# A linear-attention state gram by single heads on four column quarters of the TensorE array, with the projections around it on quarters too

## The chip, the cores and the metric

The kernel runs on one core of a Trainium2 chip. The metric is the device time of one execution in microseconds (us). A core has engines that run side by side and meet at semaphores: TensorE (PE, matmuls; PEld, its weight loads), VectorE (DVE), ScalarE (ACT), GpSimd (POOL) and SyncE (SP), which here issues most transfers. Sixteen DMA engines move the data.

## The reference, cut to what matters

Sequence 2048, width 640, 32 heads of 20. The output is a gated mix of a linear attention with a learned feature map and a GEGLU feed-forward.

```python
q, k, v = (x @ wqkv) split into 32 heads of 20
pk = k @ w_phi                                   # per head, 20 x 20; the same for q
phi_k = concat(softmax(pk), softmax(-pk))        # 40 features
kv = einsum("bhsf,bhsd->bhfd", phi_k, v)         # the state: per head 40 x 20, summed over 2048 tokens
z  = sum over tokens of phi_k
o  = (phi_q @ kv) / (phi_q @ z + 1e-6)
a  = o @ wo
b  = (gelu(x @ w_gate) * (x @ w_up)) @ w_down
out = g * a + (1 - g) * b                        # g = sigmoid(sum(x * gate_w))
```

The state gram is what changes: `kv` and `z` together, for each tile of 128 tokens the product of 21 columns (20 of v, one of ones) by 40 features per head, accumulated over 16 tiles.

## The kernel before: the parts that matter

In the "column stage", from the first gram to the last, every matmul with 128 output rows is issued as two of 64 rows, on the two column halves of the array. The halves stream at the same time (in the trace each starts a matmul of N=512 every 215.5 ns). The gram is on halves too, three heads in one matmul (so most of its output is other heads' cross terms, never used):

```python
def mm(self, bank, c0, n, lhs, rhs, first, fin, reads):      # all projections and gate/up products
    for a, z in ((0, 64), (64, P)) if self.columns else ((0, P),):
        ... e.matmul(self.ps[a:z, bank*512+c0 : ...+n], lhs[:, a:z], rhs, ...)

def gram_groups(self):                                       # 11 groups of 3 heads (the last of 2)
    fe = 3 * self.DH
    for g in range(11):
        u = g // 2
        yield (g, 64 * (g % 2), 3 + u // 4, 2 * fe * (u % 4), ..., fe * g, min(fe, self.D - fe * g))

def gram(self, t):
    ...
    for g, a, b, c, lo, f0, nf in self.gram_groups():
        ... e.matmul(self.ps[a:a+64, b*512+c : ...+2*nf], va[:, lo:lo+64], self.Ek[:, se, :, f0:f0+nf], ...)
```

One step of the stage projects a tile of 128 tokens (v, k and a gate column), makes one 512-wide product for q, and takes the gram of the tile three steps back. VectorE normalises the softmax of k (`k_norm`) meanwhile.

The softmax here doesn't subtract the row's maximum and nothing guards it: scores larger than these inputs give would overflow.

## Time and profile before

| | before |
|---|---|
| time, median of 4 runs | 286.5 us (286.4 to 287.05) |
| span of the profiled run | 285.0 us |
| PE busy | 281.1 us, 99% |
| first gram to the first recorded full-width matmul after the last gram | 28.44 to 84.44, 56.00 us |
| a steady step (one token tile, one gram) | 4.09 us |
| DMA engines | full until about 45 us (feed-forward weights from 23 us on), then nearly idle |

PE is the bottleneck from end to end, so time taken from it anywhere should come off the total. The next fence is the chain of waits of the kernel before in order of time, in a steady step (start, us, what). L361 is `mm`, L468 the gram.

```profile
52.04 0.27 PE ps L468 x8
52.30 0.05 PE ps L361
52.35 0.04 PE ps L468
52.39 3.73 PE ps L361 x37
56.12 0.27 PE ps L468 x8
```

The chain goes from matmul to matmul with nothing between, 4.08 us from gram to gram, of which the gram has about 0.3. A single matmul of the gram lasts 215 ns in the groups by shape, but matmuls are pipelined, and it is the distance of starts that tells its cost: 52.5 ns on one half for N=120, 35 ns for N=80.

Last, what follows the stage: in the timeline, the state's copies out of PSUM on VectorE (L482) and ScalarE (L484), and the next two gelus (L653):

```profile
85.64 1.34 DVE L482 CAST Ek<-ps 64x480 bf16<-64x480 f32 x2
87.08 0.82 ACT L484 ACTIVATE Ek<-ps 64x120 bf16<-64x120 f32 x3 [2.46 <-DVE Ek L482]
87.80 1.06 ACT L653 ACTIVATE gl<-ps 128x512 bf16<-128x512 f32 x2
```

### The profile page before, as it was taken

The page shows a single profiled execution, that of the slowest core. Times are in us where ns is not written, and L with a number is a line of the kernel's source. Part 1 is how long each engine was busy: PE and PEld are TensorE (multiplying, and loading weights), DVE is VectorE, ACT ScalarE, POOL GpSimd, SP SyncE. Part 2 cuts the span into 40 slices and gives each one's busy share as a digit, 9 for nine tenths or more (in the row PEclk, how much of TensorE's full clock was granted, in tenths as well). Part 3 has the DMA queues.
Part 4 walks back from the last instruction along what each step waited for, and adds up shares of the span by engine and source line. Part 5 has one row for each costly group of instructions (what it writes and reads, how often), then busy time and mean ns, then how long its engine had stood idle before and what let it go on. Part 6 is the DMA issues. An engine that isn't in the chain of part 4 may idle for free.

```text
span 285.0 us, 7066 instructions
## 1 busy us (share of the span) xinstructions
PE 281.1 (99%) x3045; PEld 186.1 (65%) x3060; DVE 174.4 (61%) x352; ACT 105.2 (37%) x200; POOL 5.3 (2%) x36
## 2 busy tenths in 40 slices
PE   8999999999999999999999999999999999999996
PEld 4665799999984444444444444445777777777786
DVE  1459999999976652667242334225883883883801
ACT  4367898667754223222322223221112112112021
POOL 7000000000000000000000000000000000000000
DMA  8999993000002000011000000000233223322421
GB/s 228 225 199 313 361 349 111 2 0 2 2 0 48 0 0 2 2 23 25 0 0 0 2 0 0 0 2 0 26 82 58 50 62 59 70 52 68 71 72 48
DMA packets 36937, 18.67 MB, mean 66 GB/s; under 512 B 28970, under 2 KB 36394, under 8 KB 36906
## 3 DMA queue, kind: packets, MB, share of 16 engines
q1 hardware_dynamic: 36240, 18.19, 26.3%
q8 instruction: 24, 0.39, 0.6%
q10 hardware_dynamic: 666, 0.03, 0.2%
q14 instruction: 7, 0.06, 0.1%
HBM read 9.04 MB, written 2.62 MB: 41 GB/s over the span
## 4 chain that ended last, share of the span: by engine, by line
PE 99%; issue 0%; ACT 0%
PE ps L361 62%; PE ps L737 28%; PE ps L681 2%; PE ps L373 2%; PE ps L468 2%; PE ps L341 1%; PE ps L557 1%; PE ps L298 0%; ACT outsb L750 0%; PE ps L564 0%; PE ps L323 0%
## 5 line engine op out<-in xcount | busy, mean ns | idle before, releaser
L361 PE MATMUL ps<-xT,wg_sb 128*128 128x512 bf16 (+1 forms) x265 | 63.8, 379 | 0.4 <-issue 0.2
L361 PE MATMUL ps<-xT,wu_sb 128*128 128x512 bf16 (+1 forms) x263 | 63.3, 379 | 0.4
L653 ACT ACTIVATE gl<-ps 128x512 bf16<-128x512 f32 x52 | 30.9, 596 | 72.9 <-PE ps L361 70.7
L655 DVE TENSOR_TENSOR hT<-ps,gl 128x512 bf16<-128x512 f32 x39 | 26.6, 689 | 38.8 <-PE ps L361 38.7
L737 PE MATMUL ps<-wd_sb,hT 64*128 64x320 bf16 x648 | 48.5, 296 | 0.0
L361 PEld LDWEIGHTS ps<-xT,wu_sb 128*128 128x128 bf16 (+1 forms) x270 | 26.6, 99 | 29.5
L361 PEld LDWEIGHTS ps<-xT,wg_sb 128*128 128x128 bf16 (+1 forms) x270 | 26.2, 99 | 29.0 <-ACT gl L653 0.2
L361 PE MATMUL ps<-w,xT 128*64 128x512 bf16 (+6 forms) x398 | 41.5, 325 | 0.1
L750 ACT ACTIVATE outsb<-ps,Gm 128x320 bf16<-128x320 f32 (+2 forms) x31 | 14.5, 515 | 72.4 <-PE ps L737 72.4
L737 PEld LDWEIGHTS ps<-wd_sb,hT 64*128 64x128 bf16 x648 | 31.1, 94 | 12.2 <-issue 0.4
L361 PEld LDWEIGHTS ps<-w,xT 128*64 128x64 bf16 (+1 forms) x400 | 35.9, 107 | 4.5
L737 PE MATMUL ps<-wo_sb,goT 64*128 64x320 bf16 (+2 forms) x340 | 26.5, 288 | 0.0
L361 PE MATMUL ps<-xT,wq 128*64 128x512 bf16 (+1 forms) x184 | 26.0, 380 | 0.1
L438 DVE TENSOR_REDUCE Dk<-Ek 128x64 f32<-128x1280 bf16 x16 | 23.7, 1478 | 3.7 <-ACT gcol L426 3.7
L452 DVE TENSOR_TENSOR Ek<-Ek,Dk 128x640 bf16<-128x640 bf16 x32 | 25.0, 821 | 0.6
L708 DVE TENSOR_TENSOR O<-ps,RH 128x640 bf16<-128x640 f32 x32 | 24.7, 815 | 0.0
L423 ACT ACTIVATE Ek<-ps 128x640 bf16<-128x640 f32 x32 | 20.7, 703 | 4.2 <-PE ps L361 4.2
L537 ACT ACTIVATE Eq<-ps 128x512 bf16<-128x512 f32 x40 | 21.6, 607 | 0.6 <-PE ps L361 0.4
L655 DVE TENSOR_TENSOR xT<-ps,gl 128x512 bf16<-128x512 f32 x13 | 9.0, 690 | 18.2 <-PE ps L361 18.2
L737 PEld LDWEIGHTS ps<-wo_sb,goT 64*128 64x128 bf16 x340 | 16.0, 94 | 5.3
L361 PEld LDWEIGHTS ps<-xT,wq 128*64 128x64 bf16 (+1 forms) x185 | 15.4, 108 | 2.9
L737 PE MATMUL ps<-wd_sb,xT 64*128 64x320 bf16 (+2 forms) x270 | 16.0, 269 | 0.0
(71 smaller groups left out, 173.8 us busy)
## 6 DMA issues: line engine op xcount, KB each, us to landing
out_dram<-outsb SPq DMA_DIRECT2D x7, 320.0 KB, 2.3
wd_sb<-in_B_w_down_dram SPq DMA_DIRECT2D x1, 2080.0 KB, 12.9
wg_sb<-in_B_w_gate_dram SPq DMA_DIRECT2D x1, 1120.0 KB, 7.4
wu_sb<-in_B_w_up_dram SPq DMA_DIRECT2D x1, 1120.0 KB, 9.8
wg_sb<-in_B_w_gate_dram SPq DMA_DIRECT2D x1, 960.0 KB, 9.1
wu_sb<-in_B_w_up_dram SPq DMA_DIRECT2D x1, 960.0 KB, 9.3
w<-in_A_wqkv_dram SPq DMA_DIRECT2D x5, 160.0 KB, 3.6
wo_sb<-in_A_wo_dram SPq DMA_DIRECT2D x1, 800.0 KB, 8.5
```

The source lines that it names most:

```text
L361: self.sc.op("pe", lambda e: e.matmul(self.ps[a:z, bank * 512 + c0:bank * 512 + c0 + n], lhs[:, a:z], rhs, start=first, stop=fin), reads=r ...
L373: sc.op("pe", lambda e, c0=c0, n=n, bk=bk, col=col: e.matmul(self.bank(bk)[:, col:col + n], self.xT[:, kt, t * P:(t + 1) * P], self.w3[:, ...
L423: self.sc.op("act", lambda e, s=s, scale=scale: e.activation(self.Ek[:, se, s, :], self.ps[:, o:o + self.D], AF.Exp, scale=scale), reads=[ ...
L438: sc.op("dve", lambda e: e.tensor_reduce(self.Dk[:, se, 0, :].rearrange("p (s h) -> p s h", h=H), self.Ek[:, se, :, :].rearrange("p s (h d ...
L452: sc.op("dve", lambda e, v=v, r=r: e.tensor_tensor(v, v, r, ALU.mult), reads=[("Rk", se)], writes=[("Ek", se, s)])
L468: sc.op("pe", lambda e: e.matmul(self.ps[a:a + 64, b * 512 + c:b * 512 + c + 2 * nf], va[:, lo:lo + 64], self.Ek[:, se, :, f0:f0 + nf], st ...
L537: sc.op("act", lambda e, s=s, scale=scale: e.activation(self.Eq[:, s, i, b * self.BT:(b + 1) * self.BT], self.bank(bank), AF.Exp, scale=sc ...
L653: sc.op("act", lambda e: e.activation(self.gl[:, slot, :], self.bank(banks[0]), AF.Gelu_apprx_tanh), reads=[("ps", banks[0])], writes=[("g ...
L655: sc.op("dve", lambda e: e.tensor_tensor(hT, self.bank(banks[1]), self.gl[:, slot, :], ALU.mult), reads=[("ps", banks[1]), ("gl", slot)], ...
L708: dve(lambda e, o=o, f=f, s=s: e.tensor_tensor(o, V[s][:, :, :, 0:DH], f, ALU.mult), rb + [key(6 + s)], [("O", s, sl)], guard=old)
L737: sc.op("pe", lambda e: e.matmul(self.bank(bk, w), lhs, rhs, start=opens and x == 0, stop=end and not opens, skip_group_check=True), reads ...
L750: sc.op("act", lambda e: e.activation(dst, self.bank(bk, w), AF.Copy, scale=g), reads=rd, writes=wr)
```

## The change

Its intent: with one head per matmul (21 columns by 40 features) and four heads side by side on the four quarters of 32 columns, no cross terms are computed; eight rounds of N=40 take the place of six rounds, mostly of N=120. A change between halves and quarters costs time (about 0.09 us each way in experiment 5), so the projections go on quarters too.

```diff
 def mm(...):
-    for a, z in ((0, 64), (64, P)) if self.columns else ((0, P),):
+    w = 32 if self.columns else P
+    for a, z in [(a, a + w) for a in range(0, P, w)]:
         ... matmul(self.ps[a:z, ...], lhs[:, a:z], rhs, ...)

 def gram(self, t):
-    for g, a, b, c, lo, f0, nf in self.gram_groups():
-        ... matmul(self.ps[a:a+64, ... 2*nf], va[:, lo:lo+64], self.Ek[:, se, :, f0:f0+nf], ...)
+    for h in range(self.H):
+        m, a = h // 4, 32 * (h % 4)
+        ... matmul(self.ps[a:a+21, b*512+40*m : b*512+40*(m+1)], self.vaug[:, sv, h, :],
+                   self.Ek[:, se, :, 20*h:20*(h+1)], ...)

 def kv_evac(self):
-    # two VectorE copies of 64 x 480, three ScalarE copies of 64 x 120 or 64 x 80
+    for j in range(4):                                 # one copy per quarter, 21 partitions
+        src = self.ps[32*j:32*j+21, b*512 : b*512 + 16*DH]...
+        # j odd: ScalarE, j even: VectorE
```

(`kv_mask` follows the new layout.) The same work takes more instructions: a steady step goes from about 102 PE loads and matmuls to about 224.

More of the change, by code (lines that the diff above doesn't have):

```diff
@@ L453, in k_scale @@
                   reads=[("Rk", se)], writes=[("Ek", se, s)])
-    def gram_groups(self):
-        fe = 3 * self.DH
-        for g in range(11):
-            u = g // 2
-            yield (g, 64 * (g % 2), 3 + u // 4, 2 * fe * (u % 4), min(3 * g * self.DA, self.H * self.DA - 64), fe * g,
-                   min(fe, self.D - fe * g))
     def gram(self, t):
@@ L465, in gram @@
         se, sv = t % self.NSE, t % self.NSV
-        va = self.vaug[:, sv, :, :].rearrange("p h c -> p (h c)")
-        for g, a, b, c, lo, f0, nf in self.gram_groups():
+        DH, b = self.DH, self.GRB
+        for h in range(self.H):
+            m, a = h // 4, 32 * (h % 4)
             sc.op("pe", lambda e: e.matmul(
-                self.ps[a:a + 64, b * 512 + c:b * 512 + c + 2 * nf], va[:, lo:lo + 64], self.Ek[:, se, :, f0:f0 + nf],
-                start=(t == 0 and g in (0, 1, 8, 9)), stop=(t == self.NT - 1 and g in (6, 7, 9, 10)),
+                self.ps[a:a + self.DA, b * 512 + 2 * DH * m:b * 512 + 2 * DH * (m + 1)], self.vaug[:, sv, h, :],
+                self.Ek[:, se, :, DH * h:DH * (h + 1)], start=(t == 0 and m == 0), stop=(t == self.NT - 1 and m == 7),
@@ L471, in gram @@
                 skip_group_check=True),
                 reads=[("Ek", se, 0), ("Ek", se, 1), ("vaug", sv), ("vmain", sv), ("vone", sv)], writes=[("ps", b)],
-                signal=(g in (7, 10)))
+                signal=(h == self.H - 1))
     def kv_evac(self):
         sc = self.sc
-        fe = 3 * self.DH
-        def copy(ek, dst, src, b):
+        DH, b = self.DH, self.GRB
+        for j in range(4):
+            a, z = 32 * j, 32 * j + self.DA
+            dst = self.Ek[a:z, 0, :, :].rearrange("p s (m q f) -> p s m q f", q=4, f=DH)[:, :, :, j, :]
+            src = self.ps[a:z, b * 512:b * 512 + 16 * DH].rearrange("p (m s f) -> p s m f", s=2, f=DH)
@@ L480, in copy @@
             rd, wr = [("ps", b)], [("Ek", 0, 0), ("Ek", 0, 1)]
-            if ek == "d":
+            if j % 2:
+                sc.op("act", lambda e: e.activation(dst, src, AF.Copy), reads=rd, writes=wr)
+            else:
                 sc.op("dve", lambda e: e.tensor_copy(dst, src), reads=rd, writes=wr)
-            else:
-                sc.op("act", lambda e: e.activation(dst, src, AF.Copy), reads=rd, writes=wr)
-        for q in (0, 1):
-            a, z = 64 * q, 64 * q + 64
-            dst = self.Ek[a:z, 0, :, 0:8 * fe].rearrange("p s (u q f) -> p u s q f", q=2, f=fe)[:, :, :, q, :]
-            src = self.ps[a:z, 3 * 512:3 * 512 + 8 * fe].rearrange("p (u s f) -> p u s f", s=2, f=fe)
-            copy("d", dst, src, 3)
@@ L490, in kv_evac @@
-        for g, a, b, c, lo, f0, nf in self.gram_groups():
-            if b == 4:
-                src = self.ps[a:a + 64, b * 512 + c:b * 512 + c + 2 * nf].rearrange("p (s f) -> p s f", f=nf)
-                copy("a", self.Ek[a:a + 64, 0, :, f0:f0 + nf], src, b)
         sc.dma("sp", lambda e: e.dma_start_transpose(
@@ L510, in kv_mask @@
         sc = self.sc
-        lows = {g: lo for g, a, b, c, lo, f0, nf in self.gram_groups()}
         for r in (0, 1):
@@ L515, in kv_mask @@
             hlo = 16 * r + 3 * i
-            for g in range(hlo // 3, (hlo + 3) // 3 + 1):
-                h0, h1 = max(hlo, 3 * g), min(hlo + 3, 3 * g + 2)
+            for g in range(hlo // 4, (hlo + 3) // 4 + 1):
+                h0, h1 = max(hlo, 4 * g), min(hlo + 3, 4 * g + 3)
                 nh, j0 = h1 - h0 + 1, h0 - hlo
-                o = (j // 2) * P + 64 * (g % 2) + h0 * self.DA - lows[g]
+                o = (j // 2) * P + 32 * (h0 % 4)
                 dst = self.KV[a:a + 64, i, :, j0 * self.DB:(j0 + nh) * self.DB].rearrange(
                     "p s (h c) -> p s h c", c=self.DB)[:, :, :, 0:self.DA]
-                src = self.Ek[q:q + 64, 2, :, o:o + nh * self.DA].rearrange("p s (h c) -> p s h c", c=self.DA)
+                src = self.Ek[q:q + 64, 2, :, o:o + nh * 32].rearrange("p s (h c) -> p s h c", c=32)[:, :, :, 0:self.DA]
                 m = self.hmask[q:q + 64, j % 2, i, j0:j0 + nh].unsqueeze(1).unsqueeze(3).to_broadcast(
@@ L781 @@
     NUMB = 2
+    GRB = 3
     oldk = [("Ek", k, r) for k in range(4) for r in (0, 1)] + [(w, k) for w in ("Dk", "Rk") for k in range(4)] + [
```

## The prediction

> **What bounds the kernel now.** TensorE: the page gives PE 281.1 us busy of 285.0 (99%), and the chain of waits is 99% PE. Between 28.4 and 84.3 us PE works on two column halves. By the starts in the trace this stage is already at the streaming rate: each half starts a 128x512 matmul every 215.5 ns (like a full-width matmul later), a 128x257 one every 110 ns; weight loads are hidden. So the projections have nothing to gain from four quarters.
>
> **What the change removes.** A state gram is 11 matmuls on two halves, six rounds: five of N=120 at 52.5 ns and one of N=80 at 35 ns, 0.297 us. The timeline agrees: a steady token-tile step takes 4.09 us, of which projections are 15 x 215.5 + 5 x 110 = 3.78, leaving 0.31. After: 32 matmuls of N=40, eight rounds of four. From the trace (N=64 on two row halves: 28.5 ns, about N/2.4 + 2) a round is 19 ns[...]. Estimate: 0.15 to 0.20 us per gram, saving 0.10 to 0.15 us x 16, about 2.0 us, all on the PE chain.
>
> **What it adds.** (1) PE instructions: a steady step goes from about 102 matmuls and loads to about 224, one per 17.6 ns for 50 us. The fastest long stretch in the trace is 22 ns (400 instructions near the end), short bursts 7 to 14 ns. I expect issue to keep up; this is the main risk. (2) The state's eviction becomes a serial chain VectorE, ScalarE, VectorE, ScalarE (all declare one destination), 640 elements per partition each: VectorE 0.82, ScalarE 0.70 us by equal shapes in the trace, with hand-offs 3.2 to 3.4 us. Before, it was 1.34 us of VectorE and 0.82 us of ScalarE; the next gelu (87.80 to 88.40) ended 0.14 us before PE reused its bank at 88.54. It will now end about 1.1 us later, and PE stalls once, about 1.0 us.
>
> VectorE is nearly full here (3.58 us per tile against a PE step of 4.09, becoming about 3.97): still enough; its last normalisation ends at 81.8 us, so the last gram can move from 83.7 to about 81.7 but hardly further.
>
> **Sum.** 286.5 - 2.0 + 1.0 = 285.4 us. Range 284.0 to 290.0. Chances: faster by over 2% 0.02, within 2% 0.80, slower by over 2% 0.18.
>
> **What would show each step.** Right: in the timeline, four 128x512 matmuls every 215 ns, four 128x257 every 110 ns; a gram in 0.15 to 0.20 us; steady steps of 3.95 to 4.0 us; in the waits, PE idle of about 1 us for the gelu on ScalarE around 86 to 89 us, after a serial eviction of 3.3 us; everything after 95 us shifted, not stretched. Wrong: quartets over 220 ns, loads that no longer hide, PE idle named "issue" in the column stage.
>
> **What would make it wrong.** Instruction supply: over 18 ns per instruction each step stretches (25 ns would cost 1.5 us a step, some 20 us in all). Four concurrent full-height streams might not hold the full rate: [...]the trace shows only two at a time. Or the gelu has more slack than I count: then 284.4.

What is cut out of the second paragraph gave a longer distance from start to start than 19 ns, and the upper 0.20 us of the estimate for a gram came from it; the 0.15 us are eight rounds of 19 ns. The sum was 286.5 - 2.0 + 1.0, put down as 285.4 us (the rounded terms make 285.5). The 19 ns are the author's estimate, read off a line through the starts in the trace of the kernel before (N=64 every 28.5 ns, N=256 every 109, N=512 every 215.5).

## More of the kernel before

All feed-forward weights and the output weights are loaded by SyncE early, one transfer behind the other:

```python
for i, (a, b) in enumerate(((0, half), (half, 13 * P))):     # gate and up weights, in two parts of the columns
    sc.dma("sp", ... wg_sb[:, :, a:b] ...); sc.dma("sp", ... wu_sb[:, :, a:b] ...)
    ...
sc.dma("sp", ... wd_sb ...)                                  # down weights, 2.1 MB
...
sc.dma("sp", ... wo_sb ...)                                  # output weights, 0.8 MB
```

From the page of the kernel before: busy us with share of the span and count of instructions; the busy tenths of PE and of the DMA engines in 40 slices of 7.1 us; the queue over which instructions come (packets, MB, share of the DMA engines); and the chain of waits by engine.

```profile
PE 281.1 (99%) x3045; PEld 186.1 (65%) x3060; DVE 174.4 (61%) x352; ACT 105.2 (37%) x200; POOL 5.3 (2%) x36
PE   8999999999999999999999999999999999999996
DMA  8999993000002000011000000000233223322421
q8 instruction: 24, 0.39, 0.6%
PE 99%; issue 0%; ACT 0%
```

## The result, and the profile after

| | before | changed |
|---|---|---|
| time, median of 4 runs | 286.5 us (286.4 to 287.05) | 290.74 us (290.29 to 291.6) |
| ratio to before | 1 | 1.0148 (1.012 to 1.0175) |
| first gram | 28.44 | 28.74 |
| first gram to the end of the stage | 56.00 us | 60.22 us |
| from there to the end | 200.56 us | 200.69 us |

Ratios here and below are the mean time of one kernel's fast runs over that of the other's in the same rounds, so they are not quite the ratio of the medians. The stage rows come from starts in the traces. (The record of the very first full-width matmul is missing in both, so both stages end one matmul, 0.22 us, too late, and their difference stands.) They are the sharper measure, for the first 28 us, where the first inputs arrive, differ by some tenths from run to run whatever the kernel (the first gram came between 28.4 and 29.2 us in the traces of before, after, after_paced, gram_only and paced_n20). The loss lies in the column stage: 4.22 us.

The same lines of the page of the changed kernel:

```profile
PE 280.8 (97%) x3921; PEld 169.0 (58%) x3936; DVE 174.6 (60%) x348; ACT 105.3 (36%) x199; POOL 5.3 (2%) x36
PE   8999967999999999999999999999999999999996
DMA  8999994000000100010100000000222322432221
q8 instruction: 31, 0.51, 0.7%
PE 91%; DVE 4%; issue 3%; DMA 1%; SPq 0%; ACT 0%; DVEq 0%
```

PE is no busier than before, but two slices fell to 6 and 7 tenths, those from 36 to 51 us. The DMA engines are full in the first of them and in part of the second. Seven more packets of instructions came (31 for 24, of 16 KB each). The chain now has "issue", time in which the profile shows nothing that PE waited for. In order of time (L362 is `mm`, L463 the gram):

```profile
36.57 0.24 issue
36.81 0.37 PE ps L463 x32
37.19 3.54 PE ps L362 x79
40.73 0.10 PE ps L463 x13
40.84 2.44 issue
43.27 0.28 PE ps L463 x17
...
47.29 1.67 issue
48.96 0.19 PE ps L463 x2
...
52.95 0.24 PE ps L463 x32
53.19 3.81 PE ps L362 x80
56.99 0.24 PE ps L463 x30
```

Two things are to be seen. From 49 us on a step takes 4.04 us (52.95 to 56.99): the gram costs 0.24 us, and the quarters stream the projections about as fast as the halves did (four matmuls of N=512 start every 215.5 ns). Before that, PE stands still inside a gram, twice, for 2.44 and 1.67 us, and there is a third, shorter gap before the gram at 36.81. The waits of PE's loads in the stage (engine, line, what it waited for, us in total, times, longest):

```profile
PEld ps L463 <- issue: 4.7, 3, 2.5
PEld ps L463 <- DVE Dk L439: 0.8, 1, 0.8
```

The profile puts part of the gap at 36.8 down to VectorE. That reading is not sound: the VectorE instruction that it names is the sum for tile 3, and the gram that starts at 36.81 is that of tile 2, whose last normalisation had ended at 35.16 us (33.60 + 1.56 in the timeline; the profile names the increment that came last).

Counting PE's records (loads, matmuls, semaphore waits) in order of start gives another view of the same gaps:

| record of PE, changed kernel | start, us | distance from the one before, us | packet of instructions that began before it: start, took, end |
|---|---|---|---|
| 702 | 31.43 | 0.005 | 24.39, 1.15, 25.5 |
| 958 | 36.81 | 0.73 | 34.35, 1.14, 35.5 |
| 1214 | 43.27 | 2.62 | 40.86, 1.15, 42.0 |
| 1470 | 48.96 | 1.85 | 46.57, 1.09, 47.7 |
| 1726 | 53.67 | 0.19 (ordinary) | 50.01, 1.20, 51.2 |

The three gaps are 256 records apart, and a packet of 16384 bytes of the instruction queue ended 1.3 us before PE went on, each time. Over the whole run, too, that queue has one packet for about 256 of PE's matmuls and loads: 24 for 6105 in the kernel before, 31 for 7857 in the changed one (23.8 and 30.7 times 256). (The trace lacks a few matmuls: up to record 958 it has three fewer than loads. So a count can be off by some records from one run to another.)

And the end of the stage, in the timeline of the changed kernel (VectorE L481, ScalarE L479 and gelu L640):

```profile
90.22 0.48 DVE L481 CAST Ek<-ps 21x320 bf16<-21x320 f32 x1
90.79 0.43 ACT L479 ACTIVATE Ek<-ps 21x320 bf16<-21x320 f32 x1 [1.59 <-DVE Ek L481]
...
91.77 0.43 ACT L479 ACTIVATE Ek<-ps 21x320 bf16<-21x320 f32 x1 [0.56 <-DVE Ek L481]
92.23 1.08 ACT L640 ACTIVATE gl<-ps 128x512 bf16<-128x512 f32 x2
93.06 1.24 PE L362 MATMUL ps<-xT,wg_sb 128*128 128x512 bf16 x5
```

The copies are serial, as foretold, but of 320 elements, not of 640. They end 2.0 us after they begin, the next gelu at about 92.8 us, before PE needs its bank at 93.06. There is no stall.

### The profile page after: what moved, and what is told of

The parts are those of the page before. It is cut to its first block, busy times and chain, and to the rows that moved or that the text cites. A ratio compares the mean times of both kernels' runs of the same rounds, so it can differ in the third digit from the quotient of the medians.

```text
span 289.6 us, 8816 instructions
## 1 busy us (share of the span) xinstructions
PE 280.8 (97%) x3921; PEld 169.0 (58%) x3936; DVE 174.6 (60%) x348; ACT 105.3 (36%) x199; POOL 5.3 (2%) x36
## 3 DMA queue, kind: packets, MB, share of 16 engines
HBM read 9.04 MB, written 2.62 MB: 40 GB/s over the span
## 4 chain that ended last, share of the span: by engine, by line
PE 91%; DVE 4%; issue 3%; DMA 1%; SPq 0%; ACT 0%; DVEq 0%
PE ps L362 57%; PE ps L724 28%; PE ps L668 2%; PE ps L374 2%; DVE Dk L439 1%; PE ps L463 1%; DMA w<-in_A_wqkv_dram 1%; PE ps L341 1%; DVE Ek L453 1%; DVE wq L354 1%; DVE Dk L448 1%; SPq L216 0%; ACT outsb L737 0%; PE ps L323 0%; DVEq L42 0%
## 5 line engine op out<-in xcount | busy, mean ns | idle before, releaser
L362 PE MATMUL ps<-xT,wg_sb 128*128 128x512 bf16 (+1 forms) x285 | 63.6, 379 | 0.4 <-issue 0.2
L362 PE MATMUL ps<-xT,wu_sb 128*128 128x512 bf16 (+1 forms) x283 | 63.1, 379 | 0.4
L640 ACT ACTIVATE gl<-ps 128x512 bf16<-128x512 f32 x52 | 30.9, 597 | 72.9 <-PE ps L362 70.7
L362 PEld LDWEIGHTS ps<-xT,wu_sb 128*128 128x128 bf16 (+1 forms) x290 | 25.7, 98 | 30.4
L362 PEld LDWEIGHTS ps<-xT,wg_sb 128*128 128x128 bf16 (+1 forms) x290 | 25.3, 98 | 29.7
L362 PE MATMUL ps<-w,xT 128*32 128x512 bf16 (+6 forms) x718 | 40.6, 328 | 0.1
L362 PEld LDWEIGHTS ps<-w,xT 128*32 128x32 bf16 (+1 forms) x720 | 25.8, 96 | 14.6
L362 PE MATMUL ps<-xT,wq 128*32 128x512 bf16 (+1 forms) x354 | 24.8, 380 | 0.1
L684 DVE RECIPROCAL RH<-ps 128x32 f32<-128x32 f32 x16 | 5.7, 358 | 15.0 <-PE ps L668 14.9
```

The lines of the kernel that those rows point to most:

```text
L362: self.sc.op("pe", lambda e: e.matmul(self.ps[a:z, bank * 512 + c0:bank * 512 + c0 + n], lhs[:, a:z], rhs, start=first, stop=fin), reads=r ...
L640: sc.op("act", lambda e: e.activation(self.gl[:, slot, :], self.bank(banks[0]), AF.Gelu_apprx_tanh), reads=[("ps", banks[0])], writes=[("g ...
```

## The experiments

**Theory A** (from the table above). PE needs one packet of the instruction queue for every 256 of its records, called a page below, and stands still where a page begins whose packet is late; it is late while the bulk weight load fills the DMA engines. From record 702 to record 1470, with that load running (358 GB/s from 30 to 36.7 us, 365 from 36.7 to 43.2), a page took 5.4 to 6.5 us from boundary to boundary, longer than the about 4.5 us in which quarters use one up (3.9 to 4.9 us in the paced kernel below). The kernel before used one up in about 10 us. **Rival B:** the grams wait for VectorE. **Rival C:** issue on four quarters is slow in itself.

### 1. Pace the weight loads (after_paced, before_paced, after_paced5)

```diff
-for i, (a, b) in enumerate(((0, half), (half, 13 * P))):     # gate and up weights
+for i, (a, b) in enumerate(((0, half),)):                    # first parts only, as before
 ...                                                          # wd, wd13, wo loads taken out here
 # in the loop over token tiles
+            if t == 8:  load second part of wg, after ScalarE's gcol of tile 8
+            if t == 11: load second part of wu, after gcol of tile 11
 # after the last gram's kv_evac
+                self.down_loads()                             # wd, wd13, wo
```

> The changed kernel with its weight loads paced: the first halves of the gate and up weights as before, the second halves singly after token tiles 8 and 11, the down and output weights after the last gram. Theory A ([...]under the bulk weight load a page takes 5.4 to 6.5 us, and the quarters use one up in about 4.5 us): the three gaps at the page boundaries (36.8, 43.3, 49.0 us) vanish, 290.7 - 5 = 285.7 us (285.2 to 286.2), faster than the changed kernel by 1.7%. Rival B (the grams wait for VectorE's normalisation, to which the profile puts part of the waiting) and rival C (mode of four quarters itself is slow to issue): no change, 290.3 to 291.5 us, gaps stay.

> Control: the kernel before with the same paced loads. It uses a page up in about 10 us, [...]and its trace shows no gap. Theory A: unchanged, 286.2 to 286.8 us. If pacing the loads helped for another reason (operand reads, other engines), this kernel would get faster as well, by several us.

Measured: changed kernel paced 286.14 us (285.93 to 286.24), ratio to before 0.9978 (0.9963 to 0.9993). Before paced 286.52 us, ratio 0.9994 (0.9978 to 1.0011). In the paced kernel the records 958, 1214 and 1470 start without a gap, at 36.26, 40.33 and 44.23 us, so two pages are used up in 8 us and PE is not short of them. Its chain at the same place:

```profile
36.65 0.24 PE ps L472 x30
36.88 3.54 PE ps L371 x80
40.42 0.24 PE ps L472 x29
```

The stage is 55.35 us: 4.87 less than with the bulk load, 0.65 less than in the kernel before. No matmul, nothing that PE waits for and no VectorE work of the stage was altered (the one new wait is SyncE's for ScalarE, before a load), so rivals B and C fall. The control shows that pacing is worth nothing without the shortage. Nor does every load bring one: in the paced kernel the second part of the gate weights, 0.96 MB, fills the DMA engines from about 51 to 54 us; a page boundary falls into that time (53.69 us), the next packet begins 0.6 us after it, and the boundary after that (58.60 us) has no gap.

Whether the paced kernel beats the one before was asked again on another chip, in five rounds.

> The changed kernel with paced weight loads once more, in five rounds, to settle whether it beats the kernel before. Theory A with a gram of 0.24 for 0.30 us on 16 tiles: 0.6 to 0.9 us less, ratio 0.997 to 0.998, its interval below 1.

Measured: 286.45 us (285.76 to 287.23), ratio 0.9999 (0.9983 to 1.0014); the expectation was missed. The profiled execution, 285.76 us, again has a stage of 55.34 us and no gap. Of the executions at 286.75 to 287.23 us there is no trace, so what they lost is open. The 0.65 us in the stage are shown twice; a gain in the total is not settled.

### 2. Move the program against the page boundaries (after_shift)

```diff
-for n in (512, 512, 512, 512, 512, 512, 128, 128, 128):      # warm-up matmuls
+for n in (64,) * 48 + (128, 128, 128):
```

> The changed kernel with 42 more matmuls (84 more instructions) in the warm-up, in the same time: 48 of N=64 for 6 of N=512. Theory A: the gaps stay at TensorE's instructions number 958, 1214 and 1470 counted from the start, so they move 84 instructions back in the program, out of the grams into the projections before them; total about 290 to 292 us. Rival B and rival C: the gaps stay in front of and inside the grams.

Measured: 292.83 us (one run), 0.8 us above the expected range. 1.35 us of its loss to the changed kernel's trace came before the stage, which began at 30.09 us for 28.74, where the chain had waited for a load of x until 16.9 us; the stage itself took 60.94 us for 60.22. The gaps are at records 958, 1214 and 1470 again, now among the projections (0.93, 2.14 and 2.52 us from start to start). The chain, L362 being `mm` and L463 the gram:

```profile
34.27 1.90 PE ps L362 x38
36.16 0.61 issue
36.77 1.83 PE ps L362 x37
...
38.98 2.34 PE ps L362 x54
41.32 1.87 issue
43.18 1.39 PE ps L362 x25
```

The gap sits in the middle of a run of projections which wait for no one, at the same count of instructions from the start. It belongs to the page, not to the gram, and that holds for the first gap too, the one partly ascribed to VectorE.

### 3. Lengthen the load (after_traffic)

```diff
+a, b = half, 13 * P
+for _ in range(3):                                           # the same weights over again, 14 MB
+    load wg_sb[:, :, a:b], wu_sb[:, :, a:b], wd_sb[:, 0:13, :], wo_sb
```

> The changed kernel with 14 MB of weights loaded again, three times the second halves, the down and the output weights, so that the DMA engines stay full from 47 to about 85 us. Theory A: further gaps of 1 to 2.5 us at each page boundary after 1470 (1726, 1982, ... every 256), until the traffic ends: 8 to 14 us longer, 299 to 305 us. Rivals B and C: at most 0.5 us longer.

Measured: 302.97 us (one run), within the expected range. Records 1726, 1982, 2238, 2494, 2750 and 3006 have got gaps, of 1.5 to 2.3 us from start to start, and none after them. The pages start at 43.29, 50.19, 56.60, 62.99, 69.39, 76.28, 82.85 and 89.35 us: one every 6.4 to 6.9 us, for 3.9 to 4.9 in the paced kernel. Part of the chain (L370 `mm`, L471 gram):

```profile
55.29 1.31 issue
56.60 3.12 PE ps L370 x56
...
61.88 1.11 issue
```

A side effect shows in the windows (us from start to end: span, PE, PEld, DVE, ACT, POOL busy, then the granted clock, DMA share and GB/s):

```profile
42.00:43.00 1.00, 0.00 (x0) 0.00 (x0) 1.00 (x2) 0.11 (x1) 0.00 (x0) 1.00 1.07 371
44.00:45.00 1.00, 1.00 (x16) 0.47 (x12) 0.96 (x2) 0.00 (x0) 0.00 (x0) 0.50 1.07 289
```

After 2.6 us without a matmul the granted clock was 0.50 for 3.4 us (43.6 to 47.0). That need not follow: in the profiled execution of the changed kernel it stayed at 1.00 after the same gap of 2.6 us. Three of the four executions of the changed kernel have a mean clock of 0.994 as well, which is what one such stretch makes of 289 us (an estimate from the 3.4 us at 0.50 of this run, which lose 1.7). They are not slower than the one at 1.0 (290.29 to 291.6 against 290.89): if the slower clock fell there too, PE used the next page up more slowly and waited less for the one after, as record 1470 does here with 1.39 for 1.85 us. That is argued, not shown.

### 4. More instructions without quarters (before_split)

```diff
 # the kernel before, halves kept
-for a, z in ((0, 64), (64, P)): matmul(ps[a:z, c : c+n], lhs[:, a:z], rhs)
+for u, v in ((0, n//2), (n//2, n)):
+    for a, z in ((0, 64), (64, P)): matmul(ps[a:z, c+u : c+v], lhs[:, a:z], rhs[:, u:v])
 # and each gram matmul as two, one for each sign of the features
```

> The kernel before, still on two column halves and with its own layout, loads and eviction, but every matmul of the column stage cut in two along its free dimension (128x512 into two of 128x256, a gram's 128x120 into two of 128x60): about 208 TensorE loads and matmuls in a step for about 102, and not one on a quarter. The cuts themselves cost about 2.4 ns each, 0.9 us in all. Theory A (a page of 256 instructions lasts 4.8 us[...]): gaps at TensorE's instructions 958, 1214 and perhaps 1470, 1.5 to 4.5 us together, so 289 to 292 us. Rival C (four quarters are to blame): 287.2 to 287.8 us, no gap.

Measured: 291.02 us (290.97 to 291.48), ratio 1.0158 (1.0141 to 1.0174): as slow as the changed kernel, without its change. Two gaps, at records 961 and 1217, 256 apart, of 0.78 and 1.51 us from start to start, and no third (in this trace no matmul is missing up to the first gap, so its 961 is the 958 of the others):

```profile
37.18 0.59 issue
37.77 0.21 PE ps L472
...
43.25 1.27 issue
44.52 2.55 PE ps L363 x57
```

Of the 4.4 us, the chain has 1.9 as "issue". Most of the rest is the cuts themselves: a steady step takes 4.22 us (from one gram at 47.07 us to the next at 51.29) against 4.09, more than the 0.9 us in all that was expected (an estimate, whose 2.4 ns a cut are near what the trace of before gives: two starts of N=256 on two row halves, 109 ns each, are 2.5 ns more than one of N=512, 215.5). So the count of instructions alone, on halves, brings the gaps; quarters are not needed for them.

### 5. The gram alone on quarters (gram_only)

```diff
 def mm(...):
-    w = 32 if self.columns else P
+    w = 64 if self.columns else P
```

> The changed gram and eviction alone: gram on quarters, projections on halves, so TensorE changes its column mode twice per tile. About 148 instructions a step, a page in 7 us: no gaps from pages (Theory A), or one under 0.3 us. What it costs are the mode changes: entering and leaving the column stage took 0.09 and 0.28 us beyond streaming in the trace of before; 16 x 0.37 - 0.7 gives 291 to 293 us. If changing between halves and quarters is free: 286.0 us.

Measured: 288.12 us (288.01 to 288.37), ratio 1.0056 (1.0038 to 1.0074). No gap at any page boundary (a page lasts about 7 us). The changes of mode cost less than expected. The expectation's 0.28 us for leaving the column stage is too long, probably through the missing record in the trace of before: five weight loads stand there beside four full-width matmuls, and by the second load (84.23 us) the first of them started about 0.1 us after the last gram had streamed. The distance of starts around a gram shows it: the first quarter matmul comes 203 ns after the last of N=257, which occupies 110, and the first half matmul 109 ns after the last of N=40, which occupies 25. With a slower first pair after that it makes about 0.2 us per gram. The chain has 4.22 us a step for 4.09:

```profile
52.71 0.30 PE ps L463 x32
...
56.93 0.30 PE ps L463 x32
```

So a change between halves and quarters cost about 0.09 us each way in this run (203 - 110 and 109 - 25 ns); what PE does in that time, no run shows. Putting the projections on quarters too was thus right: it saves 0.18 us a step (4.22 to 4.04), if the instructions arrive.

### 6. What bounds a round of the gram (paced_n20)

```diff
 # on the paced kernel; wrong results on purpose
+ns = 2 if t == 0 else 1
-    ... self.Ek[:, se, :, 20*h:20*(h+1)]        # N = 40
+    ... self.Ek[:, se, 0:ns, 20*h:20*(h+1)]     # N = 20 from the second tile on
```

> Wrong on purpose: paced loads, quarters, and from the second tile on the gram streams only the positive half, 20 elements for 40. If a round of four is bound by a fixed distance from start to start on a quarter (25 ns in the trace), the gram still takes 0.24 us in the steady steps and the total stays near 286.1 us. If it is bound by streaming, rounds fall to about 11 ns and the gram to 0.1 us, total 284 us.

Measured: 286.34 us, results wrong as intended. In the chain of this run a gram still has 0.24 us, and the starts on one quarter are still 25 ns apart:

```profile
48.52 0.24 PE ps L473 x30
48.76 3.81 PE ps L371 x79
52.57 0.24 PE ps L473 x30
```

Half the data, the same time. A quarter started a matmul, each with its own load, every 25 ns at N=40 and at N=20, so streaming did not set it (the 11 ns of the expectation are an estimate from the same starts of the trace of before as the 19 ns of the prediction). The rate of issue over all quarters is not what sets it: in gram_only the four starts of a round lie within 8 ns (52.703 to 52.711 us), and the next round comes at 52.728. What does set the 25 ns, no run shows. Eight rounds at 25 ns are 0.20 us, which is most of the gram's 0.24.

### 7. Which load does it (after_latedown)

```diff
-wd, wd13, wo loads among the early loads
+wd, wd13, wo loads after the last gram's kv_evac
```

> The simpler mend: only the down and output weights (3.0 MB) are put off until after the last gram; all gate and up weights load as before, until about 36 us. Theory A: the page of instruction 958, [...]still comes late (gap of 0.3 to 1.0 us at 36.5); the gaps at 1214 and 1470 vanish; 286.4 to 287.1 us. If the down and output loads were not what delays the later pages, 290.7 us.

Measured: 286.57 us (286.13 to 287.65), ratio 1.0005 (0.9988 to 1.0021). The gap at record 958 is still there (0.79 us, at 36.74 us); 1214 and 1470 have none, and those pages start at 40.58 and 44.48. The stage is 55.91 us. So 3.0 MB that are not needed before about 197 us caused some 4.3 of the 4.9 us (60.22 - 55.91). Whether a page waits there for a DMA engine, for a queue or for memory, no run here separates.

How the delay divides up, in the traces: the packet itself took 1.1 us, and PE went on 1.3 us after its end; from PE's crossing of a boundary to the start of the next packet it was 2.9 to 4.1 us under load in the changed kernel (1.9 us in the kernel before, up to 4.5 us in experiments 2 and 3). Without load, in the changed kernel from record 1726 on, the packet began between 0.7 us before the crossing and 0.8 us after it. When a packet is asked for, no record shows.

## Why the prediction was wrong

It said 285.4 us, 284.0 to 290.0; the measured 290.74 lies just above, and where a gain of 1.1 us was foretold, 4.2 us were lost. Its sum was 286.5 - 2.0 + 1.0; by the stage times it should have read 286.5 - 0.65 + 4.87 + 0, which is 290.7.

- **"I expect issue to keep up": the step that failed.** The risk was seen ("Instruction supply: over 18 ns per instruction each step stretches"), but as a rate of issue, even over the whole stage. The issue rate was never short: in the paced kernel 224 instructions in about 4 us, mostly 8 ns and less apart inside a gram. What was late were the packets of the instruction queue, while the DMA engines were full, until about 47 us: PE stood still three times between 36 and 49 us. Cost: 4.87 us (60.22 for 55.35). The trace of before held the warning: the instruction packets, the boundaries every 256 records, and 1.9 us from the crossing at 35.25 us to the start of the next packet at 37.11, against nearly none at 55.5. It did not hold the size: 1.9, with the packet's 1.1 and the 1.3 us after it that only the changed kernel showed, makes 4.3 us, just under the 4.5.
- **"saving 0.10 to 0.15 us x 16, about 2.0 us": right in direction, wrong in size.** A step went from 4.09 to 4.04 or 4.05 us, not to 3.95 to 4.0; less the 3.78 us of projections that is a gram of 0.31 before and about 0.26 after, 0.65 us over 16 in the stage. (The chain's 0.24 leaves out some of the ends.) A round took 25 ns (experiment 6), where the estimate had 19, and eight make 0.20; at both ends of a gram there are some 0.06 us more.
- **"PE stalls once, about 1.0 us" for the gelu: wrong by a misread size.** The copies are of 16 x 20 = 320 elements, not of 640, and take 0.48 and 0.43 us, not 0.82 and 0.70. The serial order was right; the chain took 2.0 us, not 3.3, and the gelu made it.
- **"four 128x512 matmuls every 215 ns, four 128x257 every 110 ns": right.** The starts in the changed kernel's trace are 215.5 and 109.5 ns apart for a quartet. Four streams held the full rate, and their loads stayed hidden.
- **"VectorE ... still enough": right.** In the paced kernel the chain of the stage has no VectorE. "Everything after 95 us shifted, not stretched": right, 200.69 for 200.56 us.
- **"PE idle named 'issue' in the column stage"** was put down as the sign of being wrong, and it was.

## What to carry to other kernels

When a change multiplies the instructions of an engine, ask how fast it uses up the packets in which they come, and what else the DMA engines carry in that time. For PE here, with a packet for every 256, about 4.5 us under a load that kept the DMA engines full for some 20 us was too short and 7 us was not, and a load that filled them for 3 us did no harm. An "issue" gap that recurred every 256 instructions, whatever stood there, was in these runs a late page; shift the program by some instructions to be sure. Loads that are not needed for a long time are not free just because nobody waits for them: put them where the program runs slowly through its instructions. Here 3.0 MB that were needed only from about 197 us on, loaded early, cost some 4.3 us (experiment 7).
